# Four-row read descriptors for the loads of wq and wo, with write descriptors of one partition row

## Chip, cores and metric

The kernel runs on one core of one Trainium2 chip (trn2). The metric is the device time of one execution in microseconds (us), as the median of several runs. Most runs of one kernel agree within 0.3% (the four of the kernel before: 196.47 to 196.75 us). A ratio that is given with an interval is the mean time of one kernel's fast runs over the mean of the other's fast runs of the same rounds, so it is not quite the ratio of the medians quoted beside it. All rates are those of this one core.

## The reference

One decode step of attention with a sliding window: 32 sequences, one new token each, 32 query heads, 8 key/value heads of size 128, and a window of the last 512 of 2048 cached positions. All tensors are bf16.

```python
# x [32,1,512], k_cache and v_cache [32,8,2048,128], wq [512,4096], wo [4096,512]
W = 512                                            # min(4096, max(256, 2048 // 4))
q = (x @ wq).reshape(B, 1, 32, 128)                # per head
k, v = the last W rows of each cache, every KV head shared by 4 query heads
o = softmax(q k^T * 128 ** -0.5) v
return o.reshape(B, 1, 4096) @ wo                  # [32,1,512]
```

The windows of K and V are 33.5 MB each, wq and wo 4.2 MB each: 75.5 MB to read and very little arithmetic.

## The kernel before

All large loads are issued from one queue, SyncE's (SP), in this order: wq, then K and V of the batch entries interleaved, then wo, which reuses wq's place in SBUF. PE makes the queries from wq, transposes K chunk by chunk, makes scores, and later multiplies by V; at the end it multiplies by wo as its pieces land.

```python
nc.sync.dma_start(wq_sb[:, 0, :], wq[0:P, :]).then_inc(sem_wq[0], 16)
...
def cache_rows(cache, b, h):                       # 4 heads, 32 partitions each, 16 rows (4 KB) a partition
    return cache[b, 4 * h:4 * h + 4, SK - W:, :].rearrange("g (s r) d -> s g (r d)", s=NS)
...
for kt in range(1, DKT):                           # three more blocks of wq: 128 rows of 8 KB
    sp.dma_start(wq_sb[:, kt, :], wq[kt * P:(kt + 1) * P, :]).then_inc(sem_wq[kt], 16)
...
def load_k(b):
    if b >= NK:
        sp.wait_ge(pe_T[3], b - NK + 1)            # 6 buffers
    for h in range(2):
        sp.dma_start(K_sb[:, b % NK, h].rearrange("p r d -> p (r d)"), cache_rows(k_cache, b, h)
        ).then_inc(sem_k[b % NK][h], 16)
# load_v is of the same form, with 8 buffers
for b in range(B + LEAD):
    if b < B:
        load_k(b)
    if b >= LEAD:
        load_v(b - LEAD)
sp.wait_ge(pe_qt, 1)
for hg in range(NHG):                              # eight blocks of wo: 128 partitions of 4 KB
    sp.dma_start(wo_sb[:, hg].rearrange("p i n -> p (i n)"),
                 wo[hg * 512:(hg + 1) * 512, :].rearrange("(m i) n -> m (i n)", i=4),
    ).then_inc(sem_wo[hg], 16)
```

K and V thus move as 4 KB reads and 4 KB writes, wq as 8 KB and 8 KB, wo as 4 KB and 4 KB.

## Time and profile before

| | before |
|---|---|
| median time, 4 runs (lowest to highest) | 196.51 us (196.47 to 196.75) |
| span of the profiled run | 194.7 us |
| read from HBM | 75.5 MB |
| PE, DVE, ACT busy | 74%, 52%, 30% |

The page of the kernel before. The rows DMA and GB/s cut the span into 40 equal slices; the lines q1 and q8 give packets, MB and the packets' time as a share of 16 engines' span. q1 is the queue of the loads, q8 fetches instructions.

```profile
span 194.7 us, 6153 instructions
...
PE 144.0 (74%) x2724; PEld 114.9 (59%) x2724; DVE 102.1 (52%) x190; ACT 57.6 (30%) x70; POOL 15.0 (8%) x45
...
DMA  5999999999999999999999999999999999999960
GB/s 204 426 420 406 412 405 411 407 410 407 409 407 407 408 408 410 407 407 410 407 407 410 409 407 407 410 406 408 408 406 411 405 410 405 412 405 412 406 251 31
DMA packets 20282, 75.97 MB, mean 390 GB/s; under 512 B 2272, under 2 KB 2336, under 8 KB 19744
...
q1 hardware_dynamic: 20208, 75.54, 97.2%
q8 instruction: 22, 0.36, 0.8%
```

The DMA engines are busy from end to end at a flat rate; the busiest compute engine, PE, is busy 74% of the span. The table of stretches of the kernel before, two rows of it (the DMA share is the packets' summed time over 16 engines' time, and can pass 1 where records overlap; columns: stretch, length, busy us of PE, PEld, DVE, ACT, POOL, clock granted to PE as a share of full speed, DMA share, GB/s):

```profile
60.00:100.00 40.00, 31.71 (x580) 24.76 (x578) 24.47 (x46) 13.09 (x16) 2.37 (x7) 0.91 1.03 408
100.00:140.00 40.00, 31.33 (x591) 24.80 (x590) 23.22 (x44) 12.65 (x16) 1.79 (x7) 0.91 1.03 408
```

What the SP queue waited for, kernel before. The last two columns are the number of waits and the longest; it waits for a free K buffer (L136) or V buffer (L144) for 1.2 us in all, and the DMA share of 1.03 above shows that the DMA engines do not lack work:

```profile
SPq L136 <- PE KT_ps L243: 0.9, 2, 0.5
...
SPq L144 <- PE QO_ps L293: 0.3, 1, 0.3
```

The timeline of the kernel before, lines of PE alone: start, duration, what. PE takes up each of the four wq blocks when it lands, and then the first K:

```profile
6.20 1.01 PE L221 MATMUL PT_ps<-xT_sb,w_sb 128*128 128x32 bf16 x32 [2.16 <-DMA w_sb<-in_wq_dram]
...
8.59 1.04 PE L221 MATMUL PT_ps<-xT_sb,w_sb 128*128 128x32 bf16 x32 [1.38 <-DMA w_sb<-in_wq_dram]
...
11.09 1.03 PE L221 MATMUL PT_ps<-xT_sb,w_sb 128*128 128x32 bf16 x32 [1.46 <-DMA w_sb<-in_wq_dram]
...
13.57 1.04 PE L221 MATMUL PT_ps<-xT_sb,w_sb 128*128 128x32 bf16 x32 [1.45 <-DMA w_sb<-in_wq_dram]
...
14.94 1.87 PE L243 MATMUL KT_ps<-perm,K_sb 128*128 128x128 bf16 x16 [0.33 <-DMA K_sb<-in_k_cache_dram]
```

And its end, where PE waits for the last blocks of wo and the output follows:

```profile
190.41 0.41 PE L337 MATMUL KT_ps<-w_sb,o_sel 128*32 128x128 bf16 x16 [0.63 <-DMA w_sb<-in_wo_dram]
...
191.66 0.41 PE L337 MATMUL KT_ps<-w_sb,o_sel 128*32 128x128 bf16 x16 [0.83 <-DMA w_sb<-in_wo_dram]
...
192.12 0.59 DVE L418 CAST out_sb<-KT_ps 32x128 bf16<-32x128 f32 x2 [5.39 <-PE KT_ps L337]
```

So the DMA engines' time is the kernel's time, with wq at its head and wo at its tail. Whatever makes the transfers shorter on every engine should shorten the run by about as much; that is an inference here, which the opposite case, flat_w2, bears out below (9.6 us longer for 9.2 estimated).

### The profile page before, as it was taken

What the parts mean: (1) busy time and instruction counts of PE and PEld (TensorE: products, weight loads), DVE (VectorE), ACT (ScalarE), POOL (GpSimd) and SP (SyncE); (2) the same over time, 40 slices, a digit from 0 to 9 for tenths busy, and PEclk for the clock granted to TensorE, in tenths of its full rate; (3) what the DMA queues carried; (4) which work ended last, traced back from release to release, by engine and by line L of the source; (5) the groups of instructions that cost most, each with busy time, mean ns of one, the idle gap of its engine ahead of it and who ended that gap; (6) DMA issues with size and microseconds to landing.
All of it is one profiled execution on the core that took longest, in us unless ns stands there. A gap on an engine that the chain in (4) does not pass through costs nothing.

```text
span 194.7 us, 6153 instructions
## 1 busy us (share of the span) xinstructions
PE 144.0 (74%) x2724; PEld 114.9 (59%) x2724; DVE 102.1 (52%) x190; ACT 57.6 (30%) x70; POOL 15.0 (8%) x45
## 2 busy tenths in 40 slices
PE   0448995877897679749777988779776978937881
PEld 0337773755586567537555667557666667636760
DVE  0005778745684459533944587447943574670211
ACT  3001535622262126213252236204420352213101
POOL 8502000000020001000000000000000000000000
PEclk9999999999699978996999699979998887975558
DMA  5999999999999999999999999999999999999960
GB/s 204 426 420 406 412 405 411 407 410 407 409 407 407 408 408 410 407 407 410 407 407 410 409 407 407 410 406 408 408 406 411 405 410 405 412 405 412 406 251 31
DMA packets 20282, 75.97 MB, mean 390 GB/s; under 512 B 2272, under 2 KB 2336, under 8 KB 19744
## 3 DMA queue, kind: packets, MB, share of 16 engines
q1 hardware_dynamic: 20208, 75.54, 97.2%
q8 instruction: 22, 0.36, 0.8%
q10 hardware_dynamic: 48, 0.03, 0.1%
q14 instruction: 4, 0.03, 0.0%
HBM read 75.53 MB, written 0.03 MB: 388 GB/s over the span
## 4 chain that ended last, share of the span: by engine, by line
SPq 68%; DMA 23%; PE 5%; issue 3%; DVEq 0%; DVE 0%
SPq L144 37%; SPq L136 26%; DMA K_sb<-in_k_cache_dram 15%; DMA w_sb<-in_wo_dram 8%; SPq L155 5%; PE KT_ps L243 4%; SPq L130 1%; PE S_ps L260 1%; PE QO_ps L293 0%; PE KT_ps L337 0%; SPq L118 0%; DVEq L47 0%; DVE out_sb L418 0%
## 5 line engine op out<-in xcount | busy, mean ns | idle before, releaser
L243 PE MATMUL KT_ps<-perm,K_sb 128*128 128x128 bf16 x1024 | 75.2, 235 | 22.4 <-DMA K_sb<-in_k_cache_dram 22.2
L361 DVE COPY KT_sb<-KT_ps 128x1024 bf16<-128x1024 bf16 x96 | 63.6, 689 | 52.2 <-PE KT_ps L243 52.0
L243 PEld LDWEIGHTS KT_ps<-perm,K_sb 128*128 128x128 bf16 x1024 | 65.6, 106 | 30.0 <-DMA K_sb<-in_k_cache_dram 28.4
L435 ACT ACTIVATE KT_sb<-KT_ps 128x1024 bf16<-128x1024 bf16 x32 | 32.8, 1023 | 82.3 <-PE KT_ps L243 82.3
L293 PEld LDWEIGHTS QO_ps<-PT_sb,V_sb 128*128 128x128 bf16 x1024 | 28.3, 97 | 17.8 <-issue 13.5
L293 PE MATMUL QO_ps<-PT_sb,V_sb 128*128 128x16 bf16 x1024 | 31.1, 171 | 3.3 <-DMA V_sb<-in_v_cache_dram 1.3
L383 DVE TENSOR_SCALAR P_ex<-P_f,recip 32x512 bf16<-32x512 f32 x32 | 25.4, 793 | 1.2
L260 PE MATMUL S_ps<-KT_sb,QBD 128*32 128x512 bf16 x256 | 22.2, 428 | 0.0
L453 ACT ACTIVATE PT_sb<-PT_ps 128x1024 bf16<-128x1024 bf16 x16 | 15.5, 1021 | 19.4 <-PE PT_ps L275 19.4
L203 POOL COPY QBD<-QT_sb 128x32 bf16<-128x32 bf16 x32 | 8.5, 279 | 116.1 <-PE S_ps L260 108.1
L275 PE MATMUL PT_ps<-ident,P_ex 128*128 128x128 bf16 x128 | 9.4, 231 | 9.8 <-DVE P_ex L383 9.8
L275 PEld LDWEIGHTS PT_ps<-ident,P_ex 128*128 128x128 bf16 x128 | 7.9, 104 | 10.9 <-DVE P_ex L383 10.8
L397 DVE CAST oT_sb<-QO_ps 128x32 bf16<-128x32 f32 x32 | 9.3, 289 | 7.5 <-PE QO_ps L293 7.5
L221 PE MATMUL PT_ps<-xT_sb,w_sb 128*128 128x32 bf16 x128 | 4.1, 188 | 6.4 <-DMA w_sb<-in_wq_dram 6.4
L367 DVE TENSOR_REDUCE maxv<-S_ps 128x1 f32<-128x512 f32 x8 | 5.5, 691 | 5.4 <-PE S_ps L260 5.4
L221 PEld LDWEIGHTS PT_ps<-xT_sb,w_sb 128*128 128x128 bf16 x128 | 3.7, 104 | 6.8 <-DMA w_sb<-in_wq_dram 4.6
L443 ACT ACTIVATE P_f<-S_ps,negmax 128x512 f32<-128x512 f32 x8 | 5.5, 687 | 6.3 <-DVE negmax L369 6.3
L260 PEld LDWEIGHTS S_ps<-KT_sb,QBD 128*32 128x32 bf16 x256 | 3.9, 96 | 3.9 <-issue 1.4
L353 DVE CAST QT_sb<-PT_ps 128x512 bf16<-128x512 f32 x1 | 0.7, 691 | 10.3 <-PE PT_ps L221 10.3
L337 PE MATMUL KT_ps<-w_sb,o_sel 128*32 128x128 bf16 x128 | 3.8, 289 | 1.9 <-DMA w_sb<-in_wo_dram 1.5
L337 PEld LDWEIGHTS KT_ps<-w_sb,o_sel 128*32 128x32 bf16 x128 | 2.9, 131 | 2.7 <-DMA w_sb<-in_wo_dram 2.2
L427 ACT ACTIVATE QT_sb<-PT_ps 128x512 bf16<-128x512 f32 x1 | 0.6, 597 | 12.0 <-PE PT_ps L221 12.0
(28 smaller groups left out, 22.4 us busy)
## 6 DMA issues: line engine op xcount, KB each, us to landing
K_sb<-in_k_cache_dram SPq DMA_DIRECT2D x64, 512.0 KB, 15.6
V_sb<-in_v_cache_dram SPq DMA_DIRECT2D x64, 512.0 KB, 15.4
w_sb<-in_wq_dram SPq DMA_DIRECT2D x4, 1024.0 KB, 8.3
w_sb<-in_wo_dram SPq DMA_DIRECT2D x8, 512.0 KB, 15.4
x_sb<-in_x_dram ACTq DMA_DIRECT2D x1, 32.0 KB, 2.9
out_dram<-out_sb SPq DMA_DIRECT2D x1, 32.0 KB, 1.5
```

The costliest lines, as they stand in the source:

```text
L136: sp.dma_start(K_sb[:, b % NK, h].rearrange("p r d -> p (r d)"), cache_rows(k_cache, b, h)).then_inc(sem_k[b % NK][h], 16)
L144: sp.dma_start(V_sb[:, b % NV, h].rearrange("p r d -> p (r d)"), cache_rows(v_cache, b, h)).then_inc(sem_v[b % NV], 16)
L155: sp.dma_start(wo_sb[:, hg].rearrange("p i n -> p (i n)"), wo[hg * 512:(hg + 1) * 512, :].rearrange("(m i) n -> m (i n)", i=4),).then_inc( ...
L243: ins = pe.matmul(KT_ps[:, t, i * 128:(i + 1) * 128], lhsT=K_sb[:, b % NK, h, 8 * (t % 2) + i, :], rhs=perm[:, :, :], start=True, stop=Tru ...
L260: ins = pe.matmul(S_ps[32 * c:32 * c + 32, :], lhsT=QBD[:, b % NQB, g, :], rhs=KT_sb[:, b % NKT, h, :, c, :], start=(j == 0 and h == 0), s ...
L275: ins = pe.matmul(PT_ps[:, r // 8, (r % 8) * 128:(r % 8 + 1) * 128], lhsT=P_ex[:, r, :, :].rearrange("p s g -> p (s g)"), rhs=ident[:, :], ...
L293: ins = pe.matmul(QO_ps[:, 16 * h:16 * h + 16], lhsT=V_sb[:, b % NV, h, r, :], rhs=PT_sb[:, q % 2, r, :].rearrange("p (c n) -> p c n", c=G ...
L361: dve.tensor_copy(KT_sb[:, b % NKT, t // 2, 8 * (t % 2):8 * (t % 2) + 8, :, :], KT_ps[:, t, :]).then_inc(dve_T, 1)
L383: dve.tensor_scalar(P_ex[rows, :, :, c], P_f32[rows, :].rearrange("p (r s) -> p r s", r=NR), recip[rows, q:q + 1], None, op0=ALU.mult,).th ...
L397: dve.tensor_copy(oT_sb[:, :, b], QO_ps[:, 0:HQ]).then_inc(dve_oT, 1)
L435: act.activation(KT_sb[:, b % NKT, 1, 8:16, :, :], KT_ps[:, 3, :], ACTF.Copy).then_inc(act_T, 1)
L453: act.activation(PT_sb[:, q % 2, 8 * i:8 * i + 8, :].rearrange("p r n -> p (r n)"), PT_ps[:, i, :], ACTF.Copy,).then_inc(act_PT, 1)
```

## The change

In HBM, four rows that go to four neighbouring partitions are neighbours too. The change reads them with one descriptor (32 KB for wq, 16 KB for wo), and still writes one partition row per descriptor (8 KB and 4 KB). The intent is fewer descriptors for the same bytes. The first wq block stays as it was; the new instruction is made as a copy of it with another read pattern.

```diff
-        nc.sync.dma_start(wq_sb[:, 0, :], wq[0:P, :]).then_inc(sem_wq[0], 16)
+        first = nc.sync.dma_start(wq_sb[:, 0, :], wq[0:P, :])
+        dma_form = first.ins
+        first.then_inc(sem_wq[0], 16)
+
+        def folded_load(eng, dst, src, rows):
+            src_p = eng.lower_ap_dma(src)[0]
+            n = src.ap[0][1] // rows
+            w = src.ap[0][0] * rows
+            ins = copy.replace(
+                dma_form, name=nc.get_next_instruction_name(), sync_info=None,
+                ins=[src_p.__replace__(ap=[[w, n], [1, w]])], outs=eng.lower_ap_dma(dst),
+                ant_dge_precooked=False,
+            )
+            return eng.add_instruction(ins)
...
-                sp.dma_start(wq_sb[:, kt, :], wq[kt * P:(kt + 1) * P, :]).then_inc(sem_wq[kt], 16)
+                folded_load(sp, wq_sb[:, kt, :], wq[kt * P:(kt + 1) * P, :], 4).then_inc(sem_wq[kt], 16)
...
-                sp.dma_start(
-                    wo_sb[:, hg].rearrange("p i n -> p (i n)"),
-                    wo[hg * 512:(hg + 1) * 512, :].rearrange("(m i) n -> m (i n)", i=4),
+                folded_load(
+                    sp, wo_sb[:, hg].rearrange("p i n -> p (i n)"),
+                    wo[hg * 512:(hg + 1) * 512, :].rearrange("(m i) n -> m (i n)", i=4), 4,
                 ).then_inc(sem_wo[hg], 16)
```

More of the change, by code (lines that the diff above doesn't have):

```diff
@@ L1 @@
+import copy
 from contextlib import ExitStack
```

## The prediction

> **What bounds the kernel.** The DMA engines. The page gives 75.5 MB read at a mean 390 GB/s over a 194.7 us span, PE 74% busy, DVE 52%, ACT 30%, while the slice row for DMA reads 9 nearly throughout. In the table of stretches the rate is flat, 408 GB/s from 20 to 176 us. The SP queue's own waits show only 1.2 us for buffers, so the queue is never starved[...]. At the end the engines run dry unevenly: 410 GB/s at 183-185 us, 233 at 187-188, 78 at 190-191. The last piece of wo lands at about 191.6 us, PE waits for it (0.83 us), and output follows. So the slowest DMA engine's sum of packets is the critical path, with wq at its head and wo at its tail.
>
> **What the change does.** The same bytes move between the same places in the same order. It touches 3 MB of wq (3 transfers of 1 MB) and 4 MB of wo (8 of 512 KB), 7 of 75.5 MB. Per engine a wq transfer has 2 reads of 32 KB in place of 8 of 8 KB, and a wo transfer 2 reads of 16 KB in place of 8 of 4 KB; write descriptors stay at 8 per engine. All else, K and V above all, is untouched.
>
> **Cost.** The packet records of the trace show 309 ns for 8 KB and 159 ns for 4 KB on one engine. A straight line through the two gives 27.3 bytes/ns (437 GB/s on 16 engines[...]) and about 9 ns fixed per packet. If the 9 ns belongs wholly to the read descriptor, each transfer saves 6 x 9 = 54 ns on every engine: 3 x 54 = 0.16 us for wq and 8 x 54 = 0.43 us for wo, 0.6 us together. This is an estimate and an upper bound; if the fixed part sits on the write side, or half on each, the saving is 0 to 0.3 us. All of it is on the critical path, since the engines are busy from 2 to 191 us.
>
> **Against it.** A 32 KB or 16 KB read may hold up other queues (instruction fetch: 22 packets of 16 KB, about 1.08 us each)[...]. The end of the run depends on which engines serve the fetches: each is worth 1.08 us on its engine, so a shift of one would outweigh the whole gain.
>
> **Prediction.** 196.1 us, from 195.4 to 197.0 eight times in ten. Faster by over 2%: 0.02. Within 2%: 0.95. Slower by over 2%: 0.03.
>
> **What would show it.** 8 KB packets fall from 512 to 128, and 96 of 32 KB (about 1.2 us each) appear; of the 17408 of 4 KB, 1024 go and 256 of 16 KB (about 0.6 us each) appear. If the trace records write descriptors, the counts stay. The landings of successive wq blocks, now 2.48 us apart, come to 2.43; of wo, now 1.28, to 1.22. K and V stay at 408 GB/s. PE's first transposes of K begin at about 14.8 in place of 14.94 us.
>
> **What would make it wrong.** Long reads with short writes [...]that use fewer engines: wq would then take several us more and wo would land late. Or a slowest engine that gets one fetch more or less.

The sum stays 3 x 54 + 8 x 54 ns = 0.16 + 0.43 us, 0.6 us at most. The 437 GB/s is an estimate from the two packet durations, 309 and 159 ns. That a shift of one fetch would outweigh the gain is an estimate too, from the fetches' 1.08 us (22 packets of 16 KB, median 1.083 us in the kernel before); the trace does not name the engine that serves one.

## The result

| | before | after |
|---|---|---|
| median, 4 runs each | 196.51 us | 196.56 us (196.37 to 196.63) |
| ratio, 95% interval | | 1.0003 (0.9988 to 1.0017) |

No change in time. The result is correct. The page of the kernel after:

```profile
span 194.8 us, 6153 instructions
...
DMA  5999999999999999999999999999999999999950
GB/s 198 454 391 406 412 404 410 405 415 400 412 405 407 412 404 410 405 409 407 410 405 408 409 407 407 409 409 407 408 411 405 409 406 408 409 408 426 411 229 27
DMA packets 19226, 75.97 MB, mean 390 GB/s; under 512 B 2272, under 2 KB 2336, under 8 KB 18720
...
q1 hardware_dynamic: 19152, 75.54, 97.0%
q8 instruction: 22, 0.36, 0.8%
```

The change did take effect: 1056 packets fewer, which is 3 x 96 for wq (128 reads become 32) and 8 x 96 for wo. The mean rate is the same 390 GB/s. (The higher 454 and the lower 391 beside it are bookkeeping: a long packet's bytes are counted where it starts.) The SP queue of the changed kernel waited 8.4 us for buffers in place of 1.2:

```profile
SPq L158 <- PE QO_ps L307: 6.8, 7, 1.2
SPq L150 <- PE KT_ps L257: 1.6, 2, 1.1
```

It cost nothing that shows, since rate and DMA share stayed as they were. The middle of the run is the same, from the table of stretches of the kernel after:

```profile
60.00:100.00 40.00, 31.98 (x576) 25.46 (x573) 24.11 (x46) 12.75 (x16) 1.86 (x7) 0.87 1.03 407
100.00:140.00 40.00, 32.74 (x581) 26.95 (x574) 23.19 (x43) 12.59 (x16) 1.79 (x7) 0.85 1.03 408
```

The timeline of the kernel after, PE at the start. The four wq blocks and the first K are taken up within 0.02 us of the times before:

```profile
6.21 1.02 PE L235 MATMUL PT_ps<-xT_sb,w_sb 128*128 128x32 bf16 x32 [2.17 <-DMA w_sb<-in_wq_dram]
...
8.61 1.04 PE L235 MATMUL PT_ps<-xT_sb,w_sb 128*128 128x32 bf16 x32 [1.38 <-DMA w_sb<-in_wq_dram]
...
11.09 1.04 PE L235 MATMUL PT_ps<-xT_sb,w_sb 128*128 128x32 bf16 x32 [1.45 <-DMA w_sb<-in_wq_dram]
...
13.59 1.04 PE L235 MATMUL PT_ps<-xT_sb,w_sb 128*128 128x32 bf16 x32 [1.46 <-DMA w_sb<-in_wq_dram]
...
14.95 1.86 PE L257 MATMUL KT_ps<-perm,K_sb 128*128 128x128 bf16 x16 [0.32 <-DMA K_sb<-in_k_cache_dram]
```

And the end, with the last blocks of wo taken up within 0.04 us of before:

```profile
190.38 0.62 PE L351 MATMUL KT_ps<-w_sb,o_sel 128*32 128x128 bf16 x16 [0.62 <-DMA w_sb<-in_wo_dram]
...
191.62 0.62 PE L351 MATMUL KT_ps<-w_sb,o_sel 128*32 128x128 bf16 x16 [0.62 <-DMA w_sb<-in_wo_dram]
...
192.29 0.59 DVE L432 CAST out_sb<-KT_ps 32x128 bf16<-32x128 f32 x2 [6.17 <-PE KT_ps L351]
```

So the last landing came 0.04 us earlier, and no gain of 0.4 to 0.6 us was hidden there. The output began 0.17 us later (192.29 in place of 192.12 us), because PE's last 16 products took 0.62 us in place of 0.41; the granted clock from 191 to 192 us was 0.50 in place of 1.00.

The trace also holds each packet's duration and, for each transfer, the 16 completions of the DMA engines, without saying which engine sent which. "First engine" is the earliest of the 16, "last engine" the latest. Worked out from them, for the two kernels:

| | before | after |
|---|---|---|
| wq packet, median | 8 KB: 309 ns | 32 KB: 1223 ns (4 x 309 = 1236) |
| wo packet, median | 4 KB: 159 to 161 ns | 16 KB: 639 ns (4 x 159 = 636) |
| mean distance of successive wq landings, last engine | 2.487 us | 2.488 us |
| the same for wo, first engine | 1.274 us | 1.273 us |

There is a packet record for each read. A read of four rows lasts about as long as four single ones, and transfers land at the same pace (taken the other way, wq on the first engine 2.483 and 2.489 us, wo on the last 1.256 and 1.257). That is no overhead removed and none added. The count of 8 descriptors per engine is 128 over 16 engines, as the trace does not name a packet's engine; it fits the pace. A transfer also has 16 packets of 4 B, as many as completions (2272 for 142 transfers, median 9 ns; the expectation of flat_r8w8 calls one a completion write), and 8 x 309 + 9 ns is 2.48 us, 8 x 159 + 9 ns 1.28. The question for the experiments is why.

### The profile page after: what moved, and what is told of

Same layout as the page of the kernel before. It is cut to its first block, busy times and chain, and to the rows that moved or that the text cites. A ratio compares the mean times of both kernels' runs of the same rounds, so it can differ in the third digit from the quotient of the medians.

```text
span 194.8 us, 6153 instructions
## 1 busy us (share of the span) xinstructions
PE 146.1 (75%) x2724; PEld 118.3 (61%) x2724; DVE 102.4 (53%) x190; ACT 57.6 (30%) x70; POOL 14.0 (7%) x45
## 2 busy tenths in 40 slices
DMA packets 19226, 75.97 MB, mean 390 GB/s; under 512 B 2272, under 2 KB 2336, under 8 KB 18720
## 4 chain that ended last, share of the span: by engine, by line
DMA 48%; SPq 32%; PE 15%; issue 2%; DVE 2%; DVEq 0%
DMA K_sb<-in_k_cache_dram 38%; SPq L158 16%; SPq L150 11%; DMA w_sb<-in_wo_dram 9%; PE KT_ps L257 9%; SPq L119 5%; PE QO_ps L307 2%; PE S_ps L274 2%; DVE P_ex L397 2%; PE PT_ps L289 1%; PE KT_ps L351 0%; DVEq L48 0%; DVE oT_sb L411 0%; DVE out_sb L432 0%; DVE KT_sb L375 0%
## 5 line engine op out<-in xcount | busy, mean ns | idle before, releaser
L257 PE MATMUL KT_ps<-perm,K_sb 128*128 128x128 bf16 x1024 | 76.3, 238 | 19.9 <-DMA K_sb<-in_k_cache_dram 19.4
L257 PEld LDWEIGHTS KT_ps<-perm,K_sb 128*128 128x128 bf16 x1024 | 67.7, 108 | 26.4 <-DMA K_sb<-in_k_cache_dram 25.2
L289 PE MATMUL PT_ps<-ident,P_ex 128*128 128x128 bf16 x128 | 11.0, 254 | 10.0 <-DVE P_ex L397 10.0
L289 PEld LDWEIGHTS PT_ps<-ident,P_ex 128*128 128x128 bf16 x128 | 9.4, 115 | 11.0 <-DVE P_ex L397 11.0
L217 POOL COPY QBD<-QT_sb 128x32 bf16<-128x32 bf16 x32 | 7.6, 250 | 115.8 <-PE S_ps L274 107.8
```

The costliest lines, as they stand in the source:

```text
L257: ins = pe.matmul(KT_ps[:, t, i * 128:(i + 1) * 128], lhsT=K_sb[:, b % NK, h, 8 * (t % 2) + i, :], rhs=perm[:, :, :], start=True, stop=Tru ...
L289: ins = pe.matmul(PT_ps[:, r // 8, (r % 8) * 128:(r % 8 + 1) * 128], lhsT=P_ex[:, r, :, :].rearrange("p s g -> p (s g)"), rhs=ident[:, :], ...
```

## The experiments

The expected saving was 0.6 us at most, too close to the noise. So most runs apply the same idea, or its opposite, to K and V, where 128 transfers make 9 ns on a descriptor worth several us. To fold K and V, four neighbouring partitions must be neighbours in HBM; in this kernel they hold rows of four heads, which lie 512 KB apart in the caches. The "flat" kernels therefore read, in place of four heads' windows, one head's 2048 contiguous rows: the same bytes, the same work, and **a wrong result**. They share one loader, in which read and write patterns are given apart. From here on the edits are shown in short form, not as literal code; where one side's pattern has more dimensions, a dimension of length 1 is put into the other:

```python
def raw_load(eng, dst, src, src_ap=None, dst_ap=None):   # as folded_load, patterns as given
```

Three theories. T1: what costs the fixed 9 ns is a write descriptor, and reads are free as long as there are no more of them than writes. T2: a read descriptor costs it, and the gain was hidden by something at the end of the run. T3: each side has half.

### flat_44: the control

```diff
-  cache[b, 4 * h:4 * h + 4, SK - W:, :].rearrange("g (s r) d -> s g (r d)", s=NS)
+  cache[b, 4 * h, :, :].rearrange("(p r) d -> p (r d)", p=P)      # 128 x 4 KB, contiguous
```

> Control, wrong result on purpose: each K and V transfer reads one contiguous 512 KB of its cache (all 2048 rows of one head) in place of 128 KB of each of four heads, still as 128 reads of 4 KB and 128 writes of 4 KB. Every theory: within 0.5% of the kernel before (196 to 197 us); successive K landings 1.28 us apart in the first transfers.

Measured: 196.14 us, ratio to before 0.9991 (0.9975 to 1.0008); successive landings 1.28 us apart. The control stands for the kernel before. Its stretch, as in the table above:

```profile
60.00:100.00 40.00, 32.24 (x582) 26.27 (x578) 24.44 (x46) 12.93 (x16) 2.27 (x7) 0.87 1.03 407
```

And a line of its page:

```profile
DMA packets 20282, 75.97 MB, mean 391 GB/s; under 512 B 2272, under 2 KB 2336, under 8 KB 19744
```

### flat_r16: the change's idea on all of K and V

```diff
-  reads  [[2048, 128], [1, 2048]]     # 128 of 4 KB
+  reads  [[8192, 32], [1, 8192]]      # 32 of 16 KB; writes stay 128 of 4 KB
```

> The control with the reads of all 128 K and V transfers folded to 16 KB (4 rows), writes left at 4 KB; wrong result on purpose. T1 (the fixed part of a packet is set by the write side): no change, within 0.5 us of flat_44, landings still 1.28 us apart. T2 (fixed part on the read, 9 ns each, but the end of the run hid the gain, for instance by the slowest engine's instruction fetches): 128 x 54 ns = 6.9 us less than flat_44, about 189.6 us, landings 1.23 us apart. T3 (half on each side): 3.5 us less. A record of about 640 ns per 16 KB read, as in the changed kernel, goes with T1.

Measured: 196.34 us, 0.2 us more than the control, ratio to before 0.9996 (0.9978 to 1.0014). From the table of stretches and the page of this run:

```profile
60.00:100.00 40.00, 32.87 (x572) 26.80 (x574) 23.86 (x45) 12.60 (x15) 1.88 (x7) 0.83 1.01 408
```

```profile
DMA packets 7994, 75.97 MB, mean 390 GB/s; under 512 B 2272, under 2 KB 2336, under 8 KB 3360
```

12,288 read descriptors went away and the time stayed within the noise. The 16 KB records have a median of 640 ns, and landings are 1.28 us apart. T2 (6.9 us) and T3 (3.5 us) both fall here.

### flat_w2: shorter writes

```diff
-  writes [[.., 128], [1, 2048]]              # 128 of 4 KB
+  writes [[.., 128], [1024, 2], [1, 1024]]   # 256 of 2 KB; reads stay 128 of 4 KB
```

> The control with reads of 4 KB left and every K and V write cut into two of 2 KB; wrong result on purpose. T1: 8 more write descriptors per engine and transfer at 9 ns, 128 transfers: 9.2 us more than flat_44, about 205.7 us; landings about 1.35 us apart. T2: no change. T3: 4.6 us more.

Measured: 205.71 us, 9.6 us more than the control (ratio to before 1.0477, 1.0459 to 1.0495). Divided by 128 transfers x 8 descriptors per engine this is 9.3 ns each. From this run's table of stretches and page:

```profile
60.00:100.00 40.00, 30.22 (x543) 23.81 (x539) 20.76 (x40) 10.90 (x14) 1.85 (x7) 0.87 1.03 386
```

```profile
DMA packets 20282, 75.97 MB, mean 372 GB/s; under 512 B 2272, under 2 KB 2336, under 8 KB 19744
```

The packet count is the control's to the last one, which shows that the records count reads. But the record of an unchanged 4 KB read grew from 161 to 173 ns. So in these runs the records are counted by the reads, while their length went with the writes: 173 ns for two of 2 KB, 161 for one of 4 KB. T2 (no change) and T3 (4.6 us) fall again.

### flat_r2w2: both sides shorter

```diff
+  reads  [[2048, 128], [1024, 2], [1, 1024]]   # 256 of 2 KB
+  writes [[.., 128], [1024, 2], [1, 1024]]     # 256 of 2 KB
```

> The control with reads and writes both cut to 2 KB; wrong result on purpose. T1: the same as flat_w2 (about 9.2 us more than flat_44), the number of reads making no odds. T2: 9.2 us more. T3: 9.2 us more, twice what flat_w2 adds. So flat_r2w2 equal to flat_w2 speaks for T1 and against T3.

Measured: 205.60 us, the same as flat_w2 (205.71). From its table of stretches and page:

```profile
60.00:100.00 40.00, 30.25 (x515) 23.86 (x512) 20.21 (x39) 10.35 (x14) 1.54 (x7) 0.83 1.05 386
```

```profile
DMA packets 36666, 75.97 MB, mean 373 GB/s; under 512 B 2272, under 2 KB 2336, under 8 KB 36128
```

16,384 more reads cost nothing once the writes are that many. T1 stands. T3 is out here too: it needed this run to lose twice what flat_w2 lost.

The opposite, reads shorter than writes, is not among the runs. So no run here says whether a read descriptor would cost something where reads outnumber writes. T1 may therefore also be read as "the slower side sets the pace"; the runs do not tell the two apart. For loads whose reads are no shorter than their writes, as all here, it makes no difference.

### flat_r8w8 and flat_r32w8: longer writes, and folding on top

Each K and V load becomes one transfer of 1 MB, with 8 KB per partition.

```diff
-  two transfers of 128 x 4 KB
+  flat_r8w8:  one transfer, reads [[4096, 128], [1, 4096]], writes 128 of 8 KB
+  flat_r32w8: one transfer, reads [[16384, 32], [1, 16384]], writes 128 of 8 KB
```

> As flat_44, wrong result on purpose, but K and V come in one transfer of 1 MB for both halves, 128 reads and 128 writes of 8 KB, so half as many write descriptors. T1: per engine 8 x 309 ns and one completion write of 9 ns in place of 16 x 159 and two of 9, that is 81 ns less per MB, 64 transfers: 5.2 us less than flat_44, about 191 us; successive K landings 2.48 us per MB in place of 2.56.

> As flat_r8w8 with the reads folded to 32 KB, writes left at 8 KB, wrong result on purpose: wq's form of the change on 64 transfers. T1: the same time as flat_r8w8 within 0.5 us, landings 2.48 us per MB. T2, had it been right: 64 x 54 ns = 3.5 us less than flat_r8w8.

Measured: 192.75 us and 192.39 us, ratios to before 0.9814 (0.9801 to 0.9826) and 0.9803 (0.9788 to 0.9818). The first is 3.4 us less than flat_44. The last wo block lands 4.5 us earlier (186.7 in place of 191.2 us), near the expected 5.2; some of that is lost again between there and the output, so the time missed the expected 191 us by 1.75. The tables of stretches, flat_r8w8 first, flat_r32w8 second:

```profile
60.00:100.00 40.00, 31.01 (x593) 25.58 (x591) 24.25 (x46) 13.58 (x16) 2.06 (x8) 0.91 1.01 419
```

```profile
60.00:100.00 40.00, 31.03 (x589) 26.47 (x585) 24.21 (x46) 12.76 (x17) 2.76 (x7) 0.91 1.00 418
```

Halving the write descriptors raised the rate from 407 to 419 GB/s. This step also halves the reads, which flat_r16 showed to be free, and the number of transfers, which no run separates from it; flat_w2 is the run that changes the writes alone. Folding the reads by four on top did not raise it (418); the 0.36 us between the medians is within what T1 allowed and a tenth of T2's 3.5.

### wo_only: one part of the change alone

```diff
-  folded_load(sp, wq_sb[:, kt, :], wq[kt * P:(kt + 1) * P, :], 4).then_inc(sem_wq[kt], 16)
+  sp.dma_start(wq_sb[:, kt, :], wq[kt * P:(kt + 1) * P, :]).then_inc(sem_wq[kt], 16)
```

> The change without its wq part. T1: no change against the kernel before (within 0.3 us), wo landings 1.28 us apart on an engine. A gain and a loss in the two parts of the change that cancel would show here as more than 0.3 us either way; T1 expects none.

Measured: 196.53 us, ratio 1.0008 (0.9995 to 1.0021), correct; wo landings on the first engine 1.274 us apart. So wq's part and wo's part do not cancel each other.

### k_8k: longer writes for K, in a correct kernel

If writes are what costs, a correct kernel gains by giving K 8 KB per partition. That needs 16 partitions for each of 8 heads.

```diff
-  for h in range(2): K_sb[:, b % NK, h] <- cache_rows(k_cache, b, h)
+  K_sb[:, b % NK] <- k_cache[b, :, SK - W:, :].rearrange("g (s r) d -> s g (r d)", s=16)
```

> A version meant to be correct and faster: K alone is laid out with 16 partitions per head and all 8 heads on the partitions, so that one transfer of 1 MB per batch entry has 8 KB reads and 8 KB writes; the permutation, the transposed tile and the order in which the probabilities are read follow. V, wq, wo as in the kernel before. T1: 32 x 81 ns = 2.6 us less than the kernel before, ratio about 0.987. T2 gives the same here, since reads and writes grow together. It fails to gain if the other reading order of the probabilities slows DVE onto the critical path or if PE, which gets K in one piece, falls behind.

Measured: correct, and 298 to 314 us; the ratio of its two fast runs is 1.5233 (1.5188 to 1.5279). Its stretch:

```profile
60.00:100.00 40.00, 24.88 (x323) 20.92 (x324) 15.77 (x25) 6.82 (x8) 1.52 (x4) 0.63 1.02 243
```

The engines are as busy as ever (DMA share 1.02) and move 243 GB/s. Over the whole run, the median 8 KB packet of K took 568 ns (wq's 8 KB packets in the kernel before: 309), and V's 4 KB packets, whose transfers were not touched, 256 in place of 161. So neither reason for failing (DVE, PE) was it. Two differences from the flat kernels were left: the outer dimension of the read pattern is 16 long, and it jumps 512 KB from head to head inside. The next two runs take them one at a time.

### flat_s16 and heads_s32: which of the two

```diff
-  flat_r8w8: reads [[4096, 128], [1, 4096]]
+  flat_s16:  reads [[32768, 16], [4096, 8], [1, 4096]]         # the same addresses in the same order
+  heads_s32: reads [[4096, 32], [SK * DH, 4], [1, 4096]]       # 512 KB jumps, outer dimension 32
```

> Why k_8k took 300 us and more: its 8 KB packets took about 580 ns in place of 309. Theory A: the outer dimension of its reads is 16 long (before: 32, or 128 in the flat kernels)[...]. Theory B: its reads jump from head to head (512 KB) by 8 KB pieces, and the reads are slow. This run is flat_r8w8, wrong result on purpose, same addresses on both sides and same 8 KB descriptors, with the read side written as 16 x 8 pieces in place of 128. A: as slow as K was in k_8k or worse, 8 KB packets well over 500 ns, over 280 us, as K and V both have it. B: as flat_r8w8, about 192.8 us.

> The other half of the same question, wrong result on purpose: 8 KB reads that jump from head to head by 512 KB, 4 heads inside, but with an outer dimension of 32 as in the kernel before; one 1 MB transfer for K and one for V per batch entry. A: as flat_r8w8, about 192.8 us, 8 KB packets near 312 ns. B: as slow as k_8k or slower, over 280 us.

Measured: flat_s16 279.6 to 316.0 us (no ratio was formed, its runs differ too much, and the profiled one is slow; but its fastest run is 87 us above flat_r8w8). heads_s32: 192.78 us, ratio 0.9826 (0.9812 to 0.9840), like flat_r8w8. Stretches of flat_s16 and of heads_s32:

```profile
60.00:100.00 40.00, 24.68 (x333) 20.98 (x334) 14.39 (x27) 6.81 (x8) 1.49 (x4) 0.63 1.01 235
```

```profile
60.00:100.00 40.00, 32.90 (x630) 27.41 (x627) 24.45 (x46) 14.00 (x17) 3.18 (x9) 0.87 1.01 419
```

The same addresses and the same descriptor sizes run at 235 GB/s when the read pattern is written as 16 x 8, and at 419 when it is written as 128. (The 235 comes from a run of the slow state; the fast one, at 279.58 us against 192.75, shows the same by its time.) The jumps cost nothing here, and neither does a read pattern of three dimensions: heads_s32 has both, and takes 192.78 us against 192.75 for flat_r8w8. So the outer dimension of 16 is what the slow kernels have and the fast ones have not, as theory A, in the expectation of flat_s16, said. What the runs show is that the packets take longer: 568 ns in k_8k and 542 in flat_s16 against 312 in flat_r8w8 (medians of the packets of K, or of K and V). By what means the outer dimension does this is not shown, since the trace does not name the engine of a packet. Why the times of these two kernels vary by 5% and 13% from run to run, and why k_8k, with K alone in this form, is as slow as flat_s16, stays open.

### k_quad and k_quad2: K with 8 KB writes and an outer dimension of 32

A piece of K is now 128 keys of all 8 heads of four batch entries; the 32 heads lie evenly in HBM, so they make an outer dimension of 32 with four pieces of 8 KB inside.

```diff
+  reads [[SK * DH, 32], [32 * DH, 4], [1, 32 * DH]]; writes 128 of 8 KB     # per piece t of a group q
+  scores: 32 matmuls of 128 columns per piece in place of 8 of 512
   k_quad:  exponentials written in key order, P_ex filled in another order
   k_quad2: the score matmuls write their columns in the old order; exponentials and P_ex as before
```

> A second version meant to be correct and faster: K comes in pieces of 128 keys of all 8 heads of four batch entries, 1 MB a piece, so that its outer dimension is 32 (heads) with 4 pieces of 8 KB inside; reads and writes of 8 KB. Scores are made piece by piece (32 matmuls of 128 columns in place of 8 of 512), the exponentials are written in key order. V, wq and wo as before. If A and T1 hold: 32 x 81 ns = 2.6 us less than the kernel before, ratio about 0.987. Over 280 us if B holds. It may gain less if PE, DVE[...] holds it up.

> k_quad with its one known fault mended: its DVE operation that fills P_ex had to read and write in another order and took 1373 ns in place of 793, which held PE up at every quad and at the end. Here the score matmuls write their columns straight into the order of the kernel before, so exponentials and P_ex are as before. T1 (8 KB writes for K, 2.6 us of DMA time less) and compute off the path again: 193.5 to 194.5 us, ratio 0.985 to 0.992, P_ex back at about 793 ns, wo landed by about 189.5 us. If the strided writes of the score matmuls cost PE much (over 1 us per piece), no gain.

k_quad: correct, 206.35 us, ratio 1.0543 (1.0512 to 1.0574): slower. Its DMA was fine (8 KB packets 314 ns), but this group of instructions (busy us, mean ns, idle before) was not; the kernel before first, k_quad second:

```profile
L383 DVE TENSOR_SCALAR P_ex<-P_f,recip 32x512 bf16<-32x512 f32 x32 | 25.4, 793 | 1.2
```

```profile
L402 DVE TENSOR_SCALAR P_ex<-P_f,recip 32x512 bf16<-32x512 f32 x32 | 43.9, 1373 | 1.2
```

PE's transposes of the probabilities wait for it in every group of four, 24.6 us in all (9.8 before), and once more at the end.

k_quad2: correct, 195.31 us, ratio 0.9977 (0.9950 to 1.0004). The mended operation is back at 799 ns:

```profile
L402 DVE TENSOR_SCALAR P_ex<-P_f,recip 32x512 bf16<-32x512 f32 x32 | 25.6, 799 | 1.2
```

The median is 0.9 us below the 196.23 us of the kernel before beside it, but the interval reaches from a gain of 0.5% to none, and the expected 0.985 to 0.992 was missed. Four of the six runs took 195.28 to 195.32 us, two 196.09 and 197.05. The gain did reach the DMA queue: the first engine has the last wo block 2.4 us earlier than in the kernel before (183.7 in place of 186.1 us), against 2.6 expected. The last engine has it only 1.4 us earlier (190.2 in place of 191.6). Over the whole run k_quad2 has five more instruction fetches than the kernel before (27 in place of 22), each of 16 KB and about 1.07 us on one engine; it also has 768 more matmuls, each with its weight load (7626 instructions in place of 6153):

```profile
q8 instruction: 27, 0.44, 0.9%
```

That the fetches are what spreads the engines is the author's estimate from these numbers and was not shown; the trace does not say which engine served them.

## Why the prediction was right or wrong

- **Time, range and class: right.** 196.1 us from 195.4 to 197.0 was predicted, 196.56 measured, within 2% as forecast. This tests little of the mechanism: the range is 1.6 us wide, and the whole effect in question was 0.6.
- **What bounds the kernel: right.** The changes of the write count moved the time close to what the packet records say: 9.6 us measured for 9.2 estimated in flat_w2, and 4.5 us at the last landing for 5.2 in flat_r8w8.
- **Upper bound of 0.6 us and "0 to 0.3 us" otherwise: the bound held, the middle was off.** The term that was mis-sized is "If the 9 ns belongs wholly to the read descriptor, each transfer saves 6 x 9 = 54 ns". The prediction left open which side has the 9 ns and put the central value 0.4 us below the time before. The write side has it (flat_w2 +9.6 us, flat_r16 +0.2 us), so the term measures 0 within the noise.
- **Packet counts: right.** 96 packets of 32 KB and 256 of 16 KB, 1056 packets fewer. Their durations were not: "about 0.6 us" for 16 KB came from the line through 4 and 8 KB (609 ns) and was 639; 32 KB was 1223 ns where the line gives 1209 and four writes 1236, midway; in flat_r32w8 it was 1240. The 639 and the 1240 are close to four single packets (4 x 159 = 636, 4 x 309 = 1236).
- **Landings: wrong.** "come to 2.43; of wo, now 1.28, to 1.22" was 2.488 and 1.273 us; and K's first transposes began at 14.95 us, not at "about 14.8".
- **The fears: not borne out.** Long reads with short writes did not hold up the transfers (wq's landings 2.488 us apart in place of 2.487) or other queues by anything that shows: 22 instruction fetches of 16 KB before and after, with a median of 1.083 us both times, and folding all of K and V changed the time by 0.2 us.

## What to carry to other kernels

When a kernel is bound by its DMA engines, count write descriptors, not read descriptors, as long as the reads are no more than the writes. In these runs joining reads changed nothing in four comparisons, while going from 4 KB to 8 KB per partition row was worth 3.4 us of 196 and from 4 KB to 2 KB cost 9.6 (407, 419 and 386 GB/s in flat_44, flat_r8w8 and flat_w2). When you rewrite a load's access pattern, look at the length of its outer dimension and at the packets' durations at once; the same bytes ran at 419 or at 235 GB/s (192.75 us or, in the fast run, 279.58) by that alone. To test an effect of a few ns, apply it where the kernel repeats it most, with a control of the same layout, before asking whether it pays where you wanted it.
